# Block sums of w_in and w_out formed, split and stored from one 8 KB buffer each, stores issued by ScalarE

## The chip, the cores and the metric

One core of a Trainium2 chip runs the whole kernel in one launch. The metric is the device time of an execution in microseconds (us), lower is better. TensorE (PE in the profile, PEld for its weight loads) multiplies, VectorE (DVE) and ScalarE (ACT) do the arithmetic between, SyncE (SP, its queue SPq) only issues transfers. ScalarE can issue transfers too: such a row stands as ACTq, and ScalarE does nothing else while it issues.

## The reference, cut to what matters

```python
# attention with decay lam per head, in blocks of 64 positions, gives x: 3072 tokens x 512
def _moe_ref(x, w_in, w_out):            # w_in 512 x 2048, w_out 2048 x 512
    h = x @ w_in
    g = np.maximum(h, 0.0) + np.log1p(np.exp(-np.abs(h)))     # softplus
    return g @ w_out
```

Everything is float32. The kernel keeps that precision by splitting each operand into a high part (float32r, which TensorE multiplies in one pass) and a low remainder, so a product is three matmuls: high by high, high by low, low by high.

## The kernel before, in words

The sequence is cut into six chunks of 128 positions, 512 columns each over the four batches. Chunks 0 and 1 run `x @ w_in` and `g @ w_out` plainly. Chunks 2 and 3 (the first pair) and chunks 4 and 5 (the last pair) use a seven-product scheme in place of eight block products: P1 to P7 multiply sums of blocks of x by sums of blocks of w_in. The last pair does that for w_out too. So the weights are wanted as blocks and as four sums of blocks.

**Where the sums are made.** The sums of w_in for block i (0 to 7, each covering two 128-wide slices of the 2048) go to DRAM as g1 and g2: blocks 0 to 5 are made during chunk 1, blocks 6 and 7 in steps 0 and 1 of the first pair (`block_sums` L514, `store_sums` L528, `send_sums` L573). The sums of w_out for block i are made in step i of the first pair from the tile `w2_tiles[i]` and go to DRAM as v_sums (in the profile vP), four tables that the last pair reads: `out_block_sums` L542 forms them, `out_block_high` L555 copies the high part on ScalarE, `out_block_low` L561 subtracts it on VectorE, `send_out_sums` L568 issues four stores.

**Buffers.** `t8` (L51) hands out 21 buffers of 8 KB per partition by rotation; a tile takes a buffer that an earlier tile had, and its first writer waits until that tile's last reader is through, which for a stored tile means that the store has landed. An att unit, a w1a or w1b (`load_w1` L580, read by the products), a w2 (`load_w2` L586, read by the second matmul and by the sums) and an lb tile (activations kept for chunk 3) come from the same pool. Before, a w_out block takes two of them: `full2` for the sum of the parts and the four block sums (L544), and `parts2` for high and low (L557).

**Order of work.** `tc.manual_schedule()`: each engine runs its instructions in the order in which the Python code issues them, and waits on semaphores. In one step i of the first pair (L776 to L835) TensorE runs P1, P6, P5, P2, P7, two pieces of the second matmul of the step before (`rest`), P4, P3, four pieces of `rest`, one attention unit (`event` L677), the rest of `rest`. The tile b of P6 is taken by VectorE (u2, L796) before P7 adds to the same bank, and taken again (u3, L809) before P4 does. So P7 waits for L796 and P4 for L809. Between L796 and L809 the code puts the high and low parts of the block of the step before (L798, L799), in steps 1 and 2 also those of a w_in block (L801). After the event VectorE forms the sums of step i (L828), in steps 0 and 1 also those of a w_in block (L830). The stores stand on SyncE's queue among the loads (L827, L832).

After step 7 comes the second chunk of the pair (L836 to L869): for f from 0 to 15 four pieces of the second matmul on TensorE, while ScalarE and VectorE split the kept activations two f ahead (`split` L837, high part L631 on ScalarE, low part L635 on VectorE) and prepare the blocks of x for the last pair (L596, L597). `finish` (L648) copies an output bank on ScalarE and issues its store there.

A step's time is the stretch between the starts of P1 in the trace: step 1 is 252.2 to 275.6 us, then 275.6, 297.8, 315.7, 332.9, 361.4, 379.2 start steps 2 to 7, and the second chunk runs from 393.9 to 439.0.

Of the kernel before, what the change touches and what calls it, by code (L numbers as in the profile page):

```python
# [7 lines left out]
F32 = mybir.dt.float32  # L8
# [12 lines left out]
DM = H * D  # L21
# [11 lines left out]
def decay_attention_softplus_ffn(  # L33
# [17 lines left out]
    def t8(shape, dt, name):  # L51
        return sb.tile(shape, dt, tag="b8", bufs=21, name=name)
# [192 lines left out]
    def w_of(f, which):  # L245
        j, i = divmod(w_order.index((f, which)), 2)
        return w_pairs[j][:, :, i]
# [280 lines left out]
    def store_sums(i):  # L528
        sums = block_parts.pop(i)
        parts = t8([128, 2, 4, 256], F32R, f"parts{i}")  # L530
        nc.scalar.copy(out=parts[:, 0], in_=sums)
        nc.vector.tensor_sub(out=parts[:, 1], in0=sums, in1=parts[:, 0])
        ready[i] = parts.bitcast(F32)
# [3 lines left out]


    v_sums = {p: dr.tile([128, NF // 2, 2, 256], F32, name=f"v{p}", tag=f"v{p}") for p in ("P5", "P6", "P7", "P3")}
    out_parts = {}  # L540

    def out_block_sums(i):  # L542
        w = w2_tiles[i]
        box = t8([128, 4, DM], F32, f"full2_{i}")  # L544
        full, s1, s2, s3, s4 = box[:, 0:2], *[box[:, 2 + n // 2, n % 2 * 256 : n % 2 * 256 + 256] for n in range(4)]
        nc.vector.tensor_add(out=full, in0=w[:, :, 0], in1=w[:, :, 1])
        a11, a21 = full[:, 0, 0:256], full[:, 0, 256:512]
        a12, a22 = full[:, 1, 0:256], full[:, 1, 256:512]
        nc.vector.tensor_add(out=s1, in0=a21, in1=a22)
        nc.vector.tensor_sub(out=s3, in0=a11, in1=a21)  # L550
        nc.vector.tensor_sub(out=s2, in0=s1, in1=a11)
        nc.vector.tensor_sub(out=s4, in0=a12, in1=s2)
        out_parts[i] = [box]

    def out_block_high(i):  # L555
        box = out_parts[i][0]
        parts = t8([128, 2, 4, 256], F32R, f"parts2_{i}")  # L557
        nc.scalar.copy(out=parts[:, 0].rearrange("q n c -> q (n c)"), in_=box[:, 2:4].rearrange("q n c -> q (n c)"))
        out_parts[i].append(parts)

    def out_block_low(i):  # L561
        box, parts = out_parts[i]
        nc.vector.tensor_sub(
            out=parts[:, 1].rearrange("q n c -> q (n c)"), in0=box[:, 2:4].rearrange("q n c -> q (n c)"),
            in1=parts[:, 0].rearrange("q n c -> q (n c)"),
        )

    def send_out_sums(i):  # L568
        parts = out_parts.pop(i)[1].bitcast(F32)
        for n, p in enumerate(("P5", "P6", "P7", "P3")):  # L570
            nc.sync.dma_start(out=v_sums[p][:, i], in_=parts[:, :, n])

    def send_sums(i):  # L573
        parts = ready.pop(i)
        nc.sync.dma_start(out=g1[i][:, :, 2:4], in_=parts[:, :, 0:2])
        nc.sync.dma_start(out=g2[i][:, :, 1:3], in_=parts[:, :, 2:4])
# [194 lines left out]
    nxt = 4 * NP + 1  # L771
    for c in range(STD, NCH - 2, 2):
        more = True
        lb = {}
        gs = {}
        for i in range(NF // 2):  # L776
            unit = nxt if more else None
            if unit is not None:
                load_upto(unit + 2)
            if i + 1 < NF // 2:  # L780
                load_w1(i + 1)
            load_w2(i)
            if unit is not None and unit < NG:
                k_decay(unit)
                q_decay(unit)
            if i % 2 == 0:
                l4 = t8([128, 4, 512], F32, f"lb{c}_{i}")
            for n in range(2):
                lb[2 * i + n] = l4[:, 2 * (i % 2) + n]
            ta, tb = t4([128, 2, 512], F32, f"ta{c}_{i}"), t4([128, 2, 512], F32, f"tb{c}_{i}")  # L790
            p1, u2, u3, c21 = ta[:, 0], ta[:, 1], tb[:, 0], tb[:, 1]
            a, b_ = bank(f"a{c}_{i}"), work(f"b{c}_{i}")[:, 0]
            product("P1", i, a)
            nc.scalar.copy(out=p1, in_=a)
            product("P6", i, b_)
            nc.vector.tensor_add(out=u2, in0=b_, in1=p1)  # L796
            if i >= 1:
                out_block_high(i - 1)  # L798
                out_block_low(i - 1)  # L799
            if 1 <= i <= 2:  # L800
                store_sums(NF // 2 - 3 + i)  # L801
            c_ = bank(f"c{c}_{i}")
            product("P5", i, c_)
            product("P2", i, a, False)
            la = tl([128, 512], F32, f"la{c}_{i}")
            nc.scalar.activation(la, a, AF.Softplus)
            ga = parts_of(f"g{c}_{2 * i}", la)
            product("P7", i, b_, False)
            nc.vector.tensor_add(out=u3, in0=b_, in1=p1)  # L809
            nc.vector.tensor_add(out=u3, in0=c_, in1=u3)  # L810
            nc.scalar.activation(lb[2 * i + 1], u3, AF.Softplus)
            low_of(ga, la)
            run(rest, 2)
            product("P4", i, b_, False)
            nc.vector.tensor_add(out=c21, in0=b_, in1=p1)
            nc.scalar.activation(c21, c21, AF.Softplus)
            gb = parts_of(f"g{c}_{2 * i + 1}", c21)
            product("P3", i, c_, False)
            nc.vector.tensor_add(out=u2, in0=c_, in1=u2)
            nc.scalar.activation(lb[2 * i], u2, AF.Softplus)  # L820
            run(rest, 4)
            if unit is not None and unit <= NG:
                event(unit)
                nxt += 1
            low_of(gb, c21)
            if i >= 2:
                send_out_sums(i - 2)  # L827
            out_block_sums(i)  # L828
            if i < 2:
                block_sums(NF // 2 - 2 + i)  # L830
            if 2 <= i <= 3:
                send_sums(NF // 2 - 4 + i)  # L832
            run(rest)
            pair = [(2 * i + n, (ga, gb)[n], w2_tiles[i][:, n]) for n in range(2)]
            rest = seconds(c, pair, i == NF // 2 - 1)  # L835
# [11 lines left out]
        if more:  # L847
            steps = [lambda n=n, m=m: x_block(n, xr[c + 2][:, m + (2 if n == "P2" else 0)], m) for n in ("P1", "P2") for m in range(2)]
            for n in range(2):
                steps += [lambda n=n: x_diff(c + 2, n), lambda n=n: x_diffs(c + 2, n)]  # L850
                for ps_ in (("P5", "P6"), ("P7", "P4", "P3")):
                    steps += [lambda n=n, ps_=ps_: [x_part(p, c + 2, n) for p in ps_]]
        send_out_sums(NF // 2 - 2)
        for f in range(NF - 2):
            if f == 1:
                out_block_high(NF // 2 - 1)
                out_block_low(NF // 2 - 1)
            if f == 3:
                send_out_sums(NF // 2 - 1)
            if f % 2 == 0 and f // 2 + 2 < NF // 2:  # L860
                load_w2(f // 2 + 2)
            if f + ahead < NF:
                split(f + ahead)
            if f >= 1:
                run(steps, 1)
            if f == 9 and more:
                load_w1(0)
            run(seconds(c + 1, [(f, gs.pop(f), w2_tiles[f // 2][:, f % 2])]))
# [218 lines left out]
```

## Time and profile before

| | |
|---|---|
| time, median of 3 runs | 604.32 us (603.61 to 604.48) |
| the profiled execution | 603.4 us, of it the span of instructions 601.5 us |
| busy in the span | TensorE 571.7, VectorE 393.8, ScalarE 276.9 us |
| transfers | 148.64 MB, mean 247 GB/s |
| granted TensorE clock, mean | 0.986 |

A row of the waits names an engine and line, what it waited for, the total in us, how many times, and the longest. A row of the chain or of a timeline begins with the start in us and the length in us. A row of groups gives the count, then the shortest, median and longest duration in ns, then the first and last start. A row by windows gives the stretch, its length, the busy time of each engine, the granted clock, the share of time in which the DMA engines were busy, and GB/s.

### The profile page before, as it was taken

Reading aid. Unit: us, or ns where it says so; the run is one execution under the profiler, and the core shown is the slowest. Engines: PE = TensorE matmul, PEld = TensorE weight load, DVE = VectorE, ACT = ScalarE, POOL = GpSimd, SP = SyncE. Lnnn points to the kernel's source line nnn. Section 1 sums busy time; section 2 is a strip of 40 time slices with the busy share of each in tenths; the row PEclk is TensorE's granted clock in tenths of the full one; section 3 lists DMA queues with packets and bytes.
Section 4 is the critical chain, followed back from the end, with each engine's and each line's share of the span. In section 5 each row is a group of like instructions: output and inputs, shape, how many; then the busy total and the mean of one; then the engine's idle time right before and its main releaser. Section 6 shows DMA issues by size and latency. Waiting matters only on the chain.

```text
span 601.5 us, 12196 instructions
## 1 busy us (share of the span) xinstructions
PE 571.7 (95%) x5155; PEld 463.7 (77%) x5155; DVE 393.8 (65%) x612; ACT 276.9 (46%) x446; POOL 4.6 (1%) x11
## 2 busy tenths in 40 slices
PE   8899999999999999977999669999999999999997
PEld 6577778788888887856878557888888888788886
DVE  7779998966567775667556436659313465757983
ACT  3777766844354453533343143355213343454441
POOL 3000000000000000000000000000000000000000
PEclk9999999999999999989899979999999999999999
DMA  8998556798999766748797727969945426920801
GB/s 295 405 406 301 173 207 194 267 333 326 348 395 375 243 231 233 239 172 285 246 318 283 252 82 233 305 217 370 419 148 214 151 98 207 371 118 22 294 35 70
DMA packets 52534, 148.64 MB, mean 247 GB/s; under 512 B 4480, under 2 KB 20864, under 8 KB 46464
## 3 DMA queue, kind: packets, MB, share of 16 engines
q1 hardware_dynamic: 50176, 143.68, 67.1%
q10 hardware_dynamic: 2304, 4.20, 1.9%
q8 instruction: 40, 0.66, 0.4%
q14 instruction: 14, 0.11, 0.1%
HBM read 110.10 MB, written 37.75 MB: 246 GB/s over the span
## 4 chain that ended last, share of the span: by engine, by line
PE 77%; DVE 12%; DMA 4%; ACT 3%; issue 2%; SPq 1%; DVEq 0%; ACTq 0%
PE o L643 16%; PE rP L1014 13%; PE b L624 10%; PE h L422 10%; PE o L443 8%; PE c L624 7%; PE a L624 6%; PE x L312 2%; DMA vP<-parts 2%; PE z L327 2%; DVE c L236 2%; DVE w L243 2%; PE z L331 2%; DVE c L230 2%; DMA out_dram<-ob 1%
## 5 line engine op out<-in xcount | busy, mean ns | idle before, releaser
L643 PE MATMUL o<-w,g 128*128 128x512 f32 x432 | 104.8, 395 | 0.0
L422 PE MATMUL h<-x,w 128*128 128x512 f32 x384 | 94.9, 396 | 3.1 <-DVE w L243 2.1
L643 PEld LDWEIGHTS o<-w,g 128*128 128x128 f32 x432 | 81.2, 189 | 17.3
L422 PEld LDWEIGHTS h<-x,w 128*128 128x128 f32 x384 | 70.8, 188 | 21.1 <-DVE w L243 3.8
L443 PE MATMUL o<-w,g 128*128 128x512 f32 x336 | 82.0, 392 | 1.1 <-DVE w L243 0.8
L1014 PE MATMUL rP<-sP,vP 128*128 128x512 f32 x336 | 76.3, 389 | 0.0
L443 PEld LDWEIGHTS o<-w,g 128*128 128x128 f32 x336 | 62.4, 188 | 15.0 <-DVE w L243 1.1
L1014 PEld LDWEIGHTS rP<-sP,vP 128*128 128x128 f32 x336 | 63.1, 188 | 13.1
L624 PE MATMUL b<-xcP,w1b 128*128 128x512 f32 x192 | 52.4, 410 | 17.6 <-DVE tb L809 11.9
L624 PEld LDWEIGHTS b<-xcP,w1b 128*128 128x128 f32 x192 | 37.1, 197 | 28.4 <-DVE tb L809 13.3
L624 PE MATMUL a<-xcP,w1a 128*128 128x512 f32 x192 | 48.7, 389 | 0.0
L403 ACT ACTIVATE l<-h 128x512 f32<-128x512 f32 x32 | 19.1, 597 | 59.1 <-PE h L422 56.5
L624 PEld LDWEIGHTS a<-xcP,w1a 128*128 128x128 f32 x192 | 36.0, 188 | 7.6
L411 DVE TENSOR_TENSOR g<-l,g 128x512 fp32r<-128x512 f32 x32 | 22.0, 688 | 24.7 <-ACT g L407 24.6
L339 DVE TENSOR_TENSOR a<-x,mask 128x512 f32<-128x512 f32 x15 | 10.4, 691 | 38.7 <-PE x L312 20.4
L951 DVE TENSOR_TENSOR act<-b,ta 128x512 f32<-128x512 f32 x8 | 5.5, 691 | 31.1 <-PE b L624 31.1
L624 PE MATMUL c<-xcP,w1b 128*128 128x512 f32 x96 | 25.6, 403 | 0.0
L894 ACT CAST sP<-act 128x512 fp32r<-128x512 f32 x32 | 19.2, 619 | 13.0 <-PE rP L1014 6.8
L635 DVE TENSOR_TENSOR sP<-act,sP 128x512 fp32r<-128x512 f32 x32 | 20.9, 686 | 6.6 <-ACT sP L894 6.6
L624 PE MATMUL b<-xcP,w1a 128*128 128x512 f32 x96 | 24.4, 389 | 0.0
L624 PE MATMUL c<-xcP,w1a 128*128 128x512 f32 x96 | 24.4, 389 | 0.0
L344 DVE SCALAR_TENSOR_TENSOR st<-st,lam_c,y 64x256 f32<-64x256 f32 x52 | 22.9, 480 | 0.8
(132 smaller groups left out, 869.4 us busy)
## 6 DMA issues: line engine op xcount, KB each, us to landing
att<-in_att SPq DMA_DIRECT2D x48, 512.0 KB, 7.2
w<-g SPq DMA_DIRECT2D x23, 1024.0 KB, 8.0
raw<-in_wts SPq DMA_DIRECT2D x32, 512.0 KB, 10.2
w1a<-g SPq DMA_DIRECT2D x16, 1024.0 KB, 5.2
g<-w SPq DMA_DIRECT2D x24, 512.0 KB, 8.9
w1b<-g SPq DMA_DIRECT2D x16, 768.0 KB, 6.2
g<-parts SPq DMA_DIRECT2D x16, 512.0 KB, 8.6
vP<-parts SPq DMA_DIRECT2D x32, 256.0 KB, 7.1
```

The costliest lines, as they stand in the source:

```text
L230: nc.vector.scalar_tensor_tensor(out=c, in0=raw_at(ks, 1), scalar=0x80000000, in1=c, op0=ALU.bitwise_and, op1=ALU.bitwise_or)
L236: nc.vector.tensor_add(out=c, in0=c, in1=raw_at(ks, 0))
L344: nc.vector.scalar_tensor_tensor(out=to[:, :, t], in0=of[:, :, t], scalar=lam_c[r, h : h + 1], in1=u[:, :, t], op0=ALU.mult, op1=ALU.add,)
L403: nc.scalar.activation(l_tiles[s], h_tiles.pop(s), AF.Softplus)
L411: nc.vector.tensor_sub(out=g[:, 1, :], in0=l_tiles.pop(s), in1=g[:, 0, :])
L422: nc.tensor.matmul(h_tiles[s], lhsT=w[:, i, cs], rhs=x[:, j, :], start=p == 0 and n == 0, stop=p == NP - 1 and n == 2,)
L443: nc.tensor.matmul(o_tiles[c][b], lhsT=g[:, i, b * 128 : (b + 1) * 128], rhs=w[:, j], start=f == 0 and n == 0, stop=f == NF - 1 and n == 2,)
L624: nc.tensor.matmul(to, lhsT=w[:, k, n, p * 128 : (p + 1) * 128], rhs=x[:, j, p], start=start and p == 0 and m == 0, stop=p == 1 and m == 2 ...
L635: nc.vector.tensor_sub(out=g[:, 1], in0=l, in1=g[:, 0])
L643: nc.tensor.matmul(outs[c, b], lhsT=g[:, i, b * 128 : (b + 1) * 128], rhs=w[:, j], start=f == 0 and n == 0, stop=f == NF - 1 and n == 2,)
L894: nc.scalar.copy(out=g[:, 0], in_=of)
L1014: nc.tensor.matmul(to, lhsT=w[:, k, x, n * 128 : n * 128 + 128], rhs=g[:, y], start=fresh and i == 0 and m == 0, stop=i == NF // 2 - 1 and ...
```

## The change

One tile `box` of 8 KB per block replaces `full2` and `parts2` (and for the w_in blocks 6 and 7 the two 4 KB tiles and the 8 KB tile of parts). Its first half holds the sum of the weights' parts, its second half the four block sums. Then the high parts are written over the first half, and the low parts over the block sums, in place. One box is made in each step: w_in 6 and 7 in steps 0 and 1, w_out 2 to 7 in steps 2 to 7, and w_out 0 and 1, whose w2 tiles are loaded a second time for chunk 3, in f = 2 and f = 4 of the second chunk. The high and low parts of the box of step i are made in step i + 1, its stores are issued in step i + 2, now by ScalarE.

```diff
+    def box_sums(key):
+
+        which, i = key
+        box = boxes[key] = t8([128, 4, DM], F32, f"box{which}_{i}")
+        full, (s1, s2, s3, s4) = box[:, 0:2], [box[:, 2 + n // 2, n % 2 * 256 : n % 2 * 256 + 256] for n in range(4)]
+        if which:
+            w = w2_tiles[i]
+            nc.vector.tensor_add(out=full, in0=w[:, :, 0], in1=w[:, :, 1])
+            a12, a21 = full[:, 1, 0:256], full[:, 0, 256:512]
+        else:
+            for n in range(2):
+                w = w_of(2 * i + n, 0)
+                nc.vector.tensor_add(out=full[:, n], in0=w[:, 0], in1=w[:, 1])
...
+    def box_parts(key):
+        box = boxes[key]
+        hi, lo = [box[:, 2 * n : 2 * n + 2].rearrange("q n c -> q (n c)") for n in range(2)]
+        nc.scalar.copy(out=hi.bitcast(F32R), in_=lo)
+        nc.vector.tensor_sub(out=lo.bitcast(F32R), in0=lo, in1=hi)
+
+    def box_send(key):
+        which, i = key
+        parts = boxes.pop(key).rearrange("q (k n) (m c) -> q k (n m) c", k=2, m=2)
+        if which:
+            for n, p in enumerate(("P5", "P6", "P7", "P3")):
+                nc.scalar.dma_start(out=v_sums[p][:, i], in_=parts[:, :, n])
+        else:
+            nc.scalar.dma_start(out=g1[i][:, :, 2:4], in_=parts[:, :, 0:2])
+            nc.scalar.dma_start(out=g2[i][:, :, 1:3], in_=parts[:, :, 2:4])
...
         more = True
+        box_at = [(0, NF // 2 - 2), (0, NF // 2 - 1)] + [(1, i) for i in range(2, NF // 2)]
...
             if i >= 1:
-                out_block_high(i - 1)
-                out_block_low(i - 1)
-            if 1 <= i <= 2:
-                store_sums(NF // 2 - 3 + i)
+                box_parts(box_at[i - 1])
...
             if i >= 2:
-                send_out_sums(i - 2)
-            out_block_sums(i)
-            if i < 2:
-                block_sums(NF // 2 - 2 + i)
-            if 2 <= i <= 3:
-                send_sums(NF // 2 - 4 + i)
+                box_send(box_at[i - 2])
+            box_sums(box_at[i])
...
-        send_out_sums(NF // 2 - 2)
+        box_send(box_at[NF // 2 - 2])
         for f in range(NF - 2):
-            if f == 1:
-                out_block_high(NF // 2 - 1)
-                out_block_low(NF // 2 - 1)
-            if f == 3:
-                send_out_sums(NF // 2 - 1)
+            if f in (2, 4):
+                box_sums((1, f // 2 - 1))
+            if f in (1, 3, 5):
+                box_parts((1, f // 2 - 1) if f > 1 else box_at[NF // 2 - 1])
+            if f in (3, 5, 7):
+                box_send((1, f // 2 - 2) if f > 3 else box_at[NF // 2 - 1])
```

Where the instructions now stand: ScalarE between step 5 and step 6, before the change (z is the event's output bank, v and kd belong to the attention units, ta is the copy of P1, full and parts are the block's two tiles).

```order
L387 COPY xr_3811<-z_3932 128x2x4x64
L110 COPY v_3996<-att_3651 128x512
L290 ACTIVATE kd_4021<-att_3834,rp_128 128x4x64 x2
L794 COPY ta_6_4027<-a_6_4029 128x512
L558 CAST parts_5_4045<-full_5_4003 128x1024
```

The same place of the changed kernel.

```order
L387 COPY xr_3779<-z_3899 128x2x4x64
L110 COPY v_3963<-att_3620 128x512
L573 DMA vP_641<-box_3_3608 128x2x256
L573 DMA vP_642<-box_3_3608 128x2x256
L573 DMA vP_643<-box_3_3608 128x2x256
L573 DMA vP_644<-box_3_3608 128x2x256
L290 ACTIVATE kd_3988<-att_3802,rp_128 128x4x64 x2
L800 COPY ta_6_3994<-a_6_3996 128x512
L565 CAST box_5_3970<-box_5_3970 128x1024
```

Four store issues have come in ahead of kd and of the copy of P1, and the cast reads and writes one tile.

ScalarE in the second chunk from the split of f = 4 to that of f = 7, before the change (g is a split activation, lb the kept one, xcP a block of x for the last pair).

```order
L631 CAST g_4_4422<-lb_2_3284 128x512
L596 CAST xcP_4405<-xr_3027 128x512
L631 CAST g_5_4443<-lb_2_3284 128x512
L596 CAST xcP_4446<-xr_3027 128x512
L631 CAST g_6_4463<-lb_2_3284 128x512
L596 CAST xcP_4446<-xr_3027 128x512
L631 CAST g_7_4480<-lb_2_3284 128x512
```

The end of the same place in the changed kernel, from the split of f = 6 on.

```order
L636 CAST g_6_4441<-lb_2_3266 128x512
L601 CAST xcP_4418<-xr_3027 128x512
L565 CAST box_1_4433<-box_1_4433 128x1024
L573 DMA vP_641<-box_0_4384 128x2x256
L573 DMA vP_642<-box_0_4384 128x2x256
L573 DMA vP_643<-box_0_4384 128x2x256
L573 DMA vP_644<-box_0_4384 128x2x256
L636 CAST g_7_4464<-lb_2_3266 128x512
```

A cast of a box and four stores now stand between the splits of f = 6 and f = 7; the same five stand in the same way between those of f = 4 and f = 5, with box 0 cast and box 7 stored, and four stores of box 6 stand ahead of the split of f = 2.

VectorE in the second chunk of the changed kernel, from the low part of f = 5 to that of f = 6.

```order
L640 TENSOR_TENSOR g_5_4415<-lb_2_3266,g_5_4415 128x512
L602 TENSOR_TENSOR xcP_4418<-xr_3027,xcP_4418 128x512
L549 TENSOR_TENSOR box_1_4433<-w_1_4304 128x1024
L557 TENSOR_TENSOR box_1_4433<-box_1_4433 128x256
L558 TENSOR_TENSOR box_1_4433<-box_1_4433 128x256
L559 TENSOR_TENSOR box_1_4433<-box_1_4433 128x256
L560 TENSOR_TENSOR box_1_4433<-box_1_4433 128x256
L640 TENSOR_TENSOR g_6_4441<-lb_2_3266,g_6_4441 128x512
```

The five sums of box 1 are new in that place; before, only the one xcP row stood between the two splits.

More of the change, by code (lines that the diff above doesn't have):

```diff
@@ L539, in decay_attention_softplus_ffn @@
     v_sums = {p: dr.tile([128, NF // 2, 2, 256], F32, name=f"v{p}", tag=f"v{p}") for p in ("P5", "P6", "P7", "P3")}
[L540 to L548, printed above, removed]
+    boxes = {}
+    def box_sums(key):
[10 more added lines that the diff above has]
+                nc.vector.tensor_add(out=full[:, n], in0=w[:, 0], in1=w[:, 1])
+            a12, a21 = full[:, 0, 256:512], full[:, 1, 0:256]
+        a11, a22 = full[:, 0, 0:256], full[:, 1, 256:512]
         nc.vector.tensor_add(out=s1, in0=a21, in1=a22)
@@ L552, in out_block_sums @@
         nc.vector.tensor_sub(out=s4, in0=a12, in1=s2)
[L553 to L571, printed above, removed]
+    def box_parts(key):
[12 more added lines that the diff above has]
+            nc.scalar.dma_start(out=g2[i][:, :, 1:3], in_=parts[:, :, 2:4])
     def send_sums(i):
```

## The prediction

> **What bounds the kernel now.** I read the page first, then the stretches of the first pair, then TensorE's waits there, then the chain through each wait.
>
> ```profile
> span 601.5 us, 12196 instructions
> PE 571.7 (95%) x5155; PEld 463.7 (77%) x5155; DVE 393.8 (65%) x612; ACT 276.9 (46%) x446; POOL 4.6 (1%) x11
> ```
>
> TensorE is busy 95% of the span. Only its gaps, and the time in which it ran slowly, can be won. The view by windows, cut at the starts of the steps, shows steps 1 to 7 of the first pair and the second chunk.
>
> ```profile
> core 0: us, PE busy (x) PEld busy (x) DVE busy (x) ACT busy (x) POOL busy (x), PEclk, DMA share, GB/s
> 252.20:275.60 23.40, 19.37 (x195) 15.24 (x195) 14.00 (x24) 9.50 (x16) 0.00 (x0) 0.93 0.57 192
> 275.60:297.80 22.20, 19.16 (x196) 15.35 (x195) 15.26 (x27) 8.22 (x13) 0.00 (x0) 0.92 0.79 274
> 297.80:315.70 17.90, 17.68 (x180) 14.20 (x179) 11.55 (x20) 7.19 (x12) 0.00 (x0) 1.00 0.92 316
> 315.70:332.90 17.20, 17.20 (x180) 14.25 (x179) 10.68 (x18) 7.29 (x12) 0.00 (x0) 1.00 0.73 255
> 332.90:361.40 28.50, 19.23 (x180) 15.46 (x179) 10.77 (x18) 7.17 (x12) 0.00 (x0) 0.82 0.54 175
> 361.40:379.20 17.80, 17.52 (x179) 14.19 (x179) 10.70 (x18) 6.38 (x10) 0.00 (x0) 1.00 0.81 258
> 379.20:393.90 14.70, 14.70 (x126) 12.02 (x124) 11.71 (x20) 5.38 (x8) 0.00 (x0) 1.00 0.89 299
> 393.90:439.00 45.10, 45.10 (x199) 37.35 (x200) 24.78 (x40) 20.33 (x36) 0.00 (x0) 1.00 0.86 329
> ```
>
> Step 4 (315.70) is TensorE from end to end: 17.20 us. Against it steps 1, 2, 3, 5 and 6 are long by 6.2, 5.0, 0.7, 11.3 and 0.6 us, together 23.8. Step 7 and the second chunk have no gap.
>
> ```profile
> PE b L624 <- DVE tb L809: 11.9, 3, 9.3
> PE b L624 <- DVE ta L796: 5.0, 3, 3.0
> ```
>
> These are TensorE's waits on the banks of the products, from the view of waits: 16.9 us, all for the two VectorE operations that free the bank b. The other 6.9 us is slowness: in steps 1, 2 and 5 the same products took 19.37, 19.16 and 19.23 us at clocks 0.93, 0.92 and 0.82, about 2.0 us more each. What held VectorE is in the chain.
>
> ```profile
> 252.84 7.64 DMA out_dram<-ob
> 260.58 1.06 ACT parts L558
> 261.65 1.23 DVE parts L563
> 262.88 1.13 DVE parts L532
> ...
> 339.76 1.26 SPq L571
> 341.06 6.24 DMA vP<-parts
> 347.40 1.05 ACT parts L558
> ```
>
> Step 1: ScalarE's cast into the tile of parts waits until an output store out of that buffer has landed; VectorE, in order, stands behind the cast, then does two low parts, then L809. Step 5: the same cast waits for the stores of an earlier block's parts. Step 2 is different, in the timeline of VectorE and TensorE (the last row is from step 3):
>
> ```profile
> 277.24 1.22 DVE L546 TENSOR_TENSOR full<-w 128x1024 f32<-128x1024 f32 x1
> 279.97 1.29 DVE L518 TENSOR_TENSOR full<-w 128x512 f32<-128x512 f32 x2
> 283.37 0.68 DVE L796 TENSOR_TENSOR ta<-b,ta 128x512 f32<-128x512 f32 x1
> 284.11 1.68 PE L624 MATMUL b<-xcP,w1b 128*128 128x512 f32 x6 [3.04 <-DVE ta L796]
> 303.52 1.65 PE L624 MATMUL b<-xcP,w1b 128*128 128x512 f32 x6 [0.22 <-DVE ta L796]
> ```
>
> There VectorE makes two sets of sums ahead of L796, and P7 waits 3.04 us for it. With one set, in step 3, it waits 0.22.
>
> **What goes.** The in-place cast needs no second buffer, so it can't wait for a landing. A box still needs its one buffer when the sums start, a step earlier. By the addresses of the built program, the boxes take buffers of att and w1 tiles or of blocks whose stores were issued at least a step before, and TensorE is done with those tiles before the sums begin. That ends the stops of steps 1 and 5, and the short ones of 3 and 6, where the cast waited on a w1a tile. In steps 1 and 2 one set of sums goes (277.24 to 279.97, 2.73 us) and with it one low part. In step 2, L796 then ends at 283.37 + 0.68 - 2.73 = 281.3, and P7 was ready at 284.11 - 3.04 = 281.1: 0.2 to 0.3 us stays, as in step 3. So 23.8 - 0.5 = 23.3 us go, the slow time included, since it stood behind the stops.
>
> The operations cost the same in place, by the groups on the tiles full, sums and parts:
>
> ```profile
> L523 DVE TENSOR_TENSOR sums<-full x8: 424/426/427, 142.4 to 281.3; 128x256 f32<-128x256 f32 x8
> L549 DVE TENSOR_TENSOR full<-full x8: 424/425/426, 253.7 to 392.7; 128x256 f32<-128x256 f32 x8
> L558 ACT CAST parts<-full x8: 1044/1050/1057, 260.6 to 402.5; 128x1024 fp32r<-128x1024 f32 x8
> ```
>
> A sum into its own tile (L549) takes what one into another takes (L523), so I keep 1.05 us for the cast. The low part in place has no row; I take it unchanged.
>
> **What comes in, in the steps.** Four store issues per block move from SyncE to ScalarE, between the copy of v and kd. Here is the timeline between steps 4 and 5, and two batches of stores on SyncE's queue.
>
> ```profile
> 330.94 0.62 ACT L110 COPY v<-att 128x512 f32<-128x512 f32 x1
> 331.46 0.91 ACT L290 ACTIVATE kd<-att,rp 128x256 f32<-128x256 f32 x2
> 333.64 1.22 DVE L546 TENSOR_TENSOR full<-w 128x1024 f32<-128x1024 f32 x1
> 334.34 0.59 ACT L794 COPY ta<-a 128x512 f32<-128x512 f32 x1 [1.96 <-PE a L624]
> 372.82 3.56 SPq L571 DMA_DIRECT2D vP<-parts  x4
> 404.82 2.31 SPq L571 DMA_DIRECT2D vP<-parts  x4
> ```
>
> ScalarE has no row for this issue. SyncE's four took 2.31 to 3.56 us, waits included. On ScalarE they start at 331.56, and kd takes 0.91. L794 must end before P2, three products of 1.36 into the step, at 332.9 + 4.1 = 337.0. So 337.0 - 0.59 - 0.91 - 331.56 = 3.9 us are free, and even 3.56 hides: zero. If that cover were gone, each of the six steps would pay the 2.3.
>
> **What comes in, in the second chunk.** Boxes 0 and 1 of w_out are formed here, and the stores of boxes 6, 7, 0 and 1 are issued among the splits, which TensorE needs every 2.73 us (45.10 us for 198 matmuls, twelve for each f).
>
> ```profile
> 409.52 0.68 DVE L635 TENSOR_TENSOR g<-lb,g 128x512 fp32r<-128x512 f32 x1
> ```
>
> This row of VectorE's timeline is the low part of f = 7, ready at 410.2. TensorE comes to f = 7 after 114 of those matmuls, at 419.9, and to its third matmul, which reads the low part, at 420.3: a lead of 10.1 us. Ahead of it now stand three times four stores, two sets of sums and two casts, and they don't overlap: a cast waits for the sums, the stores stand behind the cast, the next split behind the stores, the next sums behind that split's low part. With s for four stores that is 3s + 2 x 2.73 + 2 x 1.05 = 7.6 + 3s. At s = 2.31, the batch that lies in this chunk, it is 14.5, so TensorE loses 14.5 - 10.1 = 4.4 us, in gaps of about a microsecond from f = 5 to f = 7. At s = 3.56 it is 8.1. Below, nothing: if the two engines do overlap more than I think, the loss is 0. I take 4.4. What the gaps do to the clock is bounded by step 3 (no loss of clock) and step 2 (2.0 us): I take 0. The Trainium skill, "TensorE: Matmul & The Clock Gate", section "What's actually happening", says that the clock falls to half after an idle window of some 3.4 us; by it gaps of a microsecond cost no clock, and the sum stays at 4.4.
>
> **The sum.** 603.4 - 23.3 + 4.4 = 584.5 us for the profiled execution; it lies 0.9 below the median of the runs, 604.32, so 585.4 there. About 0.2% (1.2 us) can be told from no change.
>
> **The rivals.** *The second chunk covers it all.* ScalarE stood idle there 24.8 of 45.1 us, and its stores may issue faster than SyncE's. Then 604.3 - 23.3 = 581.0. Chance 0.13.
>
> *The wait moves to the loads.* Two loads now take a box's buffer after its stores: w1b of block 6 that of box 2 (with w2 of block 5 queued behind it), w2 of block 6 that of box 3. The rows are the landing times of the stores of parts, the w2 loads among the DMA issues, and a wait of SyncE's queue in the first pair.
>
> ```profile
> DMA to landing us min/median/max: 2.8/7.1/9.7
> w<-g SPq DMA_DIRECT2D x23, 1024.0 KB, 8.0
> SPq L588 <- DMA out_dram<-ob: 11.4, 2, 10.3
> ```
>
> Stores (first row) that start 1.3 us ahead of a step are out 1.0 to 2.3 us into it, landed at 8.1 (7.1) to 12.0 (9.7), and a w2 load (second row) ends at 16.1 to 20.0. VectorE wants it at 333.64 - 315.70 = 17.9 us into the step. At the median 1.8 us are left; at the worst each of the two steps loses 2.1: 585.4 + 4.2 = 589.6, with slower stores in the second chunk 593. Chance 0.15. The Trainium skill, "DMA: Bandwidth & Descriptors", section "Issuing engines are not separate DMA queues", speaks for it and against moving the stores: all issuers share the same 16 engines, and another queue saves issue time alone. By it the landings stay as long as they were; no row of before shows stores of this kind from ScalarE.
>
> *ScalarE stands in its stores: slower.* By the built program each transfer takes one of eight completion counters in turn and is not issued until that counter's last transfer has landed. The last row shows it: a w2 load stood up to 10.3 us for an output store whose buffer it doesn't share. On SyncE that delays loads; on ScalarE it stops the casts and activations. The third store of box 3, at the end of step 5, waits for the load of att unit 23. By my times that is issued as step 4 ends, a step ahead. If SyncE ran a step late, ScalarE would stand the landing of some 7 us, less the 1.6 that the cover of 3.9 leaves beside the issue, and TensorE would restart 2.0 slow: 7.4 us in each of steps 4 to 7, 29.6 in all, and 615 us. It decides from 23.3 - 4.4 = 18.9, that is 4.7 us a step. Against it: without the stores SyncE runs further ahead. Chance 0.05.
>
> *The boxes wait as the parts did*, since their buffers come from the same rotation: 604, chance 0.03.
>
> **How the numbers follow.** My forecast has 0.64: 585.4. The low end is all 23.8 us won with nothing given back, 580.5. The high end takes s = 3.56 (8.1 us), the clock's 2.0 and both late loads (4.2): 604.3 - 23.3 + 14.3 = 595.3, rounded to 595. Outside lie the last two rivals, 0.08. Faster: 0.64 + 0.13 + 0.15 = 0.92; same 0.03; slower 0.05.
>
> **What would show it.** Right: steps 1 to 6 at 17.2 to 17.6 us with clock 1.00; no wait of a box's cast for a transfer; ScalarE's copy of P1 before P2 in every step; the second chunk at 48 to 51 us, TensorE waiting there for splits of f = 4 to 9. Wrong: a first sum or an activation that waits for a landing in steps 4 to 7, a second chunk of 45.1 or of over 54 us, or stores whose issue on ScalarE differs much from 2.3 us for four.

## The result, and the profile after

The change takes the kernel from 603.97 us (median of 4 runs, 601.45 to 604.48) to 584.71 us (4 runs, 584.27 to 585.31): a ratio of 0.969 (of the means), 95% interval 0.966 to 0.9719. The forecast was 585.4. The profiled execution took 585.31 us. In the changed kernel the line numbers differ a little: VectorE's two operations that free the bank b, formerly L796 and L809, are now L802 and L812, the products of a pair L629, the second matmuls L648, the split L636 (high, ScalarE) and L640 (low, VectorE); a box is cast at L565 and stored at L573.

The page after has a span of 583.4 us. The view by windows after, cut at the starts of the steps, with the columns as before: the first row is step 1, the last the second chunk, the one ahead of it step 7.

```profile
252.30:269.60 17.30, 17.30 (x196) 14.34 (x195) 10.35 (x18) 8.68 (x15) 0.00 (x0) 1.00 0.83 295
269.60:287.40 17.80, 17.49 (x195) 14.20 (x194) 11.55 (x21) 7.27 (x12) 0.00 (x0) 1.00 0.59 209
287.40:305.20 17.80, 17.58 (x179) 14.22 (x179) 11.51 (x20) 7.41 (x13) 0.00 (x0) 1.00 0.79 278
305.20:322.40 17.20, 17.20 (x179) 14.26 (x179) 10.69 (x18) 6.72 (x11) 0.00 (x0) 1.00 0.48 175
322.40:339.70 17.30, 17.30 (x180) 14.33 (x179) 10.78 (x18) 7.16 (x12) 0.00 (x0) 1.00 0.81 290
339.70:356.90 17.20, 17.20 (x179) 14.26 (x178) 10.65 (x17) 7.40 (x12) 0.00 (x0) 1.00 0.67 230
356.90:371.60 14.70, 14.70 (x126) 12.03 (x124) 11.71 (x20) 5.38 (x8) 0.00 (x0) 1.00 0.87 325
371.60:420.90 49.30, 47.27 (x199) 36.74 (x200) 32.37 (x52) 22.22 (x38) 0.00 (x0) 1.00 0.83 293
```

Steps 1 to 6 add up to 104.6 us where they took 127.0, with the clock at 1.00 in each: 22.4 us won. The second chunk takes 49.3 where it took 45.1: 4.2 us lost. The difference, 18.2, is the difference of the spans to 0.1 (601.5 - 583.4 = 18.1). What TensorE still waits for from step 0 to the end of the second chunk, in the view of waits (total, times, longest):

```profile
PE o L648 <- DVE g L640: 1.2, 2, 0.9
PE o L648 <- ACT g L636: 0.9, 1, 0.9
PE b L629 <- DVE ta L802: 0.5, 2, 0.3
```

The old waits of 11.9 us for L809 are gone, and of the 5.0 for L796 0.5 is left, in steps 2 and 3. New are waits of the second matmuls for splits. TensorE's own timeline of the second chunk shows where (one f has twelve of these matmuls; the row at 371.53 begins with thirty that belong to the chunk before, and the stretch holds f = 0 to 13):

```profile
371.53 12.54 PE L648 MATMUL o<-w,g 128*128 128x512 f32 x54
384.95 6.46 PE L648 MATMUL o<-w,g 128*128 128x512 f32 x26 [0.88 <-ACT g L636]
391.69 6.30 PE L648 MATMUL o<-w,g 128*128 128x512 f32 x24 [0.28 <-DVE g L640]
398.86 22.05 PE L648 MATMUL o<-w,g 128*128 128x512 f32 x94 [0.87 <-DVE g L640]
```

It stops at f = 2, at the third matmul of f = 4 and at the third of f = 6. The visible gaps add up to 2.0 us. The rest of the 4.2 lies inside the rows (47.27 us busy for what took 45.10). There the weight loads of these matmuls show it, in the view of their waits:

```profile
PEld o L648 <- DVE g L640: 3.3, 5, 1.3
```

With another 2.0 us for high parts, in three waits, the loads stood 5.3 us for splits; loads run beside matmuls (37.35 us of them beside 45.10 in the second chunk before), so TensorE loses less than that. With SyncE's stores (below) the same view has no wait for a split.

ScalarE, in the view of its waits, never waits for a landing before a box's cast. It waits for VectorE's sums:

```profile
ACT box L565 <- DVE box L560: 17.6, 9, 3.1
```

### The profile page after: what moved, and what is told of

The parts are those of the page before. It is cut to its first block, busy times and chain, and to the rows that moved or that the text cites. A ratio compares the mean times of both kernels' runs of the same rounds, so it can differ in the third digit from the quotient of the medians.

```text
span 583.4 us, 12175 instructions
## 1 busy us (share of the span) xinstructions
PE 567.5 (97%) x5155; PEld 460.1 (79%) x5155; DVE 394.3 (68%) x612; ACT 277.7 (48%) x446; POOL 4.1 (1%) x11
## 4 chain that ended last, share of the span: by engine, by line
PE 74%; DVE 10%; DMA 9%; ACT 2%; ACTq 2%; issue 1%; SPq 1%; DVEq 0%
PE rP L1014 13%; PE o L648 13%; PE b L629 11%; PE h L422 10%; PE o L443 9%; PE c L629 7%; PE a L629 7%; DMA raw<-in_wts 5%; DMA g<-w 2%; PE x L312 2%; PE z L327 2%; DMA att<-in_att 2%; ACTq L573 2%; PE z L331 1%; DVE c L236 1%
## 5 line engine op out<-in xcount | busy, mean ns | idle before, releaser
L648 PE MATMUL o<-w,g 128*128 128x512 f32 x432 | 105.8, 394 | 2.0 <-DVE g L640 1.2
L648 PEld LDWEIGHTS o<-w,g 128*128 128x128 f32 x432 | 79.9, 188 | 21.8 <-DVE g L640 3.3
L629 PE MATMUL b<-xcP,w1b 128*128 128x512 f32 x192 | 49.1, 391 | 1.3 <-DVE act L951 0.8
L629 PE MATMUL a<-xcP,w1a 128*128 128x512 f32 x192 | 48.8, 389 | 0.0
L629 PEld LDWEIGHTS b<-xcP,w1b 128*128 128x128 f32 x192 | 35.8, 188 | 9.9 <-DVE ta L802 1.4
L629 PEld LDWEIGHTS a<-xcP,w1a 128*128 128x128 f32 x192 | 36.1, 188 | 7.5
L640 DVE TENSOR_TENSOR sP<-act,sP 128x512 fp32r<-128x512 f32 x32 | 20.9, 686 | 6.6 <-ACT sP L894 6.6
L629 PE MATMUL c<-xcP,w1b 128*128 128x512 f32 x96 | 24.4, 390 | 0.0
L629 PE MATMUL b<-xcP,w1a 128*128 128x512 f32 x96 | 24.4, 389 | 0.0
L629 PE MATMUL c<-xcP,w1a 128*128 128x512 f32 x96 | 24.4, 389 | 0.0
L387 ACT COPY xr<-z 128x512 f32<-128x512 f32 x16 | 9.4, 585 | 30.4 <-PE z L331 30.0
```

Source lines behind the costliest of these rows:

```text
L629: nc.tensor.matmul(to, lhsT=w[:, k, n, p * 128 : (p + 1) * 128], rhs=x[:, j, p], start=start and p == 0 and m == 0, stop=p == 1 and m == 2 ...
L640: nc.vector.tensor_sub(out=g[:, 1], in0=l, in1=g[:, 0])
L648: nc.tensor.matmul(outs[c, b], lhsT=g[:, i, b * 128 : (b + 1) * 128], rhs=w[:, j], start=f == 0 and n == 0, stop=f == NF - 1 and n == 2,)
```

## The experiments

My theory: the stops of steps 1 to 6 went because no cast takes a second buffer, and because one set of sums went from steps 0 and 1. The 4.2 us given back are the stores that ScalarE now issues and the two boxes formed among the splits. The rivals: the other queue made the gain; VectorE's sums alone make the loss; each batch of stores costs its own gap; ScalarE stands for landings.

All runs in one table. The last two columns are differences of starts in TensorE's timeline, of the first product of step 1, of step 7 and of the second pair. In the changed kernel these are 252.17, 356.75 and 420.75 us, and they are read in the same way from each of the other traces.

| kernel | median, us (runs) | steps 1-6 | step 7 and second chunk |
|---|---|---|---|
| before | 603.97 (4) | 127.0 | 59.8 |
| the change | 584.71 (4) | 104.6 | 64.0 |
| the change again, one run | 584.68 (1) | 104.6 | 63.2 |
| all box stores on SyncE | 581.70 (4) | 104.5 | 59.8 |
| all box stores on GpSimd | 582.07 (5) | 104.6 | 59.8 |
| last boxes later | 581.53 (4) | 104.5 | 59.8 |
| SyncE and later | 581.42 (5) | 104.6 | 59.8 |
| stores of boxes 5, 6 on SyncE | 581.58 (4) | 104.6 | 59.8 |
| stores of boxes 7, 0, 1 on SyncE | 583.09 (4) | 104.6 | 61.0 |
| stores of boxes 2, 3, 4 twice | 594.01 (6) | 116.1 | 63.6 |
| before, w_out in place | 589.03 (4) | 111.0 | 59.8 |
| before, all sums in place | 587.23 (5) | 110.7 | 59.8 |

The kernel before, run beside the experiments, had medians of 603.44, 603.10 and 603.62.

**The stores back on SyncE.**

```diff
-                nc.scalar.dma_start(out=v_sums[p][:, i], in_=parts[:, :, n])
+                nc.sync.dma_start(out=v_sums[p][:, i], in_=parts[:, :, n])
```

(and the two stores of w_in's boxes likewise).

> The changed kernel with every box store issued by SyncE again instead of ScalarE; nothing else differs. My theory: the stops of steps 1 to 6 ended because no cast waits for a landing any more, and the 4.2 us of the second chunk are mostly ScalarE's issuing, four batches of stores of 2.3 to 3.7 us among the splits. Then the seven steps keep their sum of 104.6 us, and the second chunk falls from 49.3 to 45.2-46.5 us, since two sets of sums and two casts (7.6 us) fit in the lead of 10.1 us: 580.7-582 us. Rival one, the other queue made the gain: with the stores on SyncE again the loads behind them come late, the steps grow by several us, 588 us or more. Rival two, VectorE's sums and the casts make the second chunk long and the issuing costs nothing: 584.7 us, the chunk at 49.

Measured: 581.70 us, ratio 0.9643 (0.963 to 0.9656). The steps are unchanged, and the second chunk is one row of TensorE's timeline, without a gap:

```profile
371.78 45.18 PE L648 MATMUL o<-w,g 128*128 128x512 f32 x198
```

So the queue made none of the gain in the steps, and both sets of sums and all casts fit in the second chunk when ScalarE issues nothing for them. Both rivals fall. The move to ScalarE, taken alone, cost 3.0 us.

**Before, with w_out's sums in place.**

```diff
-        parts = t8([128, 2, 4, 256], F32R, f"parts2_{i}")
-        nc.scalar.copy(out=parts[:, 0].rearrange("q n c -> q (n c)"), in_=box[:, 2:4].rearrange("q n c -> q (n c)"))
+        hi, lo = [box[:, 2 * n : 2 * n + 2].rearrange("q n c -> q (n c)") for n in range(2)]
+        nc.scalar.copy(out=hi.bitcast(F32R), in_=lo)
...
```

(the low part and the four stores use the same two halves).

> The kernel before with one thing of the change: the high and low parts of w_out's blocks are written into the block's own buffer, so that no second 8 KB buffer is taken. The two sets of sums in steps 0 and 1, the separate buffers of the two w_in blocks and SyncE's stores stay as before. My theory: the waits of ScalarE's cast for a landing go with the buffer, so the stops of steps 3, 5 and 6 go (0.7 + 11.3 + 0.6 us) and most of step 1's 6.2; step 2 keeps its wait for the two sets of sums (3.0 us and 2.0 of slow clock), and step 1 some 1 to 2 us; the second chunk stays at 45.1. Then 604.0 - 12.6 - 4.5 = 587 us, between 585 and 589. But the parts of the two w_in blocks still take a buffer of their own in steps 1 and 2: if their cast waits as w_out's did, step 1 keeps its whole stop and it is 591. Rival, the other queue or the order of the work made the gain: the steps stay as they were, 600 us or more.

Measured: 589.03 us, ratio 0.9764 (0.975 to 0.9779), at the upper edge of the 585 to 589 that I expected. Steps 1 and 2 took 20.9 and 20.7 us, step 3 17.8, steps 4 to 6 17.2 each. TensorE's timeline shows the waits left in steps 1 and 2, and ScalarE's the casts of step 1, that of w_out's block and that of a w_in block's parts. In this kernel L793 and L806 are the two operations that free the bank b.

```profile
260.33 1.65 PE L621 MATMUL b<-xcP,w1b 128*128 128x512 f32 x6 [1.73 <-DVE ta L793]
264.66 1.65 PE L621 MATMUL b<-xcP,w1b 128*128 128x512 f32 x6 [1.32 <-DVE tb L806]
282.50 1.66 PE L621 MATMUL b<-xcP,w1b 128*128 128x512 f32 x6 [3.04 <-DVE ta L793]
```

```profile
256.24 1.05 ACT L558 CAST full<-full 128x1024 fp32r<-128x1024 f32 x1 [0.65 <-DVE full L552]
261.70 1.05 ACT L531 CAST parts<-sums 128x1024 fp32r<-128x1024 f32 x1 [4.41 <-DMA att<-in_att]
```

The cast in place (L558) starts as soon as its sums are there. The cast beside it, which still takes a second buffer (L531), stands 4.41 us for a landing. (The row names the transfer that landed last; by the built program the cast waits for the four output stores out of the buffer that it takes.) The two forms of the same work, in one step of one kernel, show the mechanism. The 11.3 us that step 5 was long are gone with the second buffer alone, without anything else of the change.

**Before, with all sums in place.** The order and the queue of before, with the changed kernel's box functions.

```diff
-                out_block_high(i - 1)
-                out_block_low(i - 1)
+                box_parts((1, i - 1))
             if 1 <= i <= 2:
-                store_sums(NF // 2 - 3 + i)
+                box_parts((0, NF // 2 - 3 + i))
```

> The kernel before with all block sums of the first pair formed, split and stored in one buffer each, the two of w_in too, but in the order of before: two sets of sums in steps 0 and 1, two parts in steps 1 and 2, every store from SyncE. The run with w_out alone in place (589.0) kept 3.6 us in step 1 and 3.5 in step 2; in step 1 TensorE waited 1.7 us behind the double sums and 1.3 behind the cast of the w_in parts, which stood for a landing. My theory: the second wait goes with the buffer, the first and that of step 2 (3.0 us) stay, since they are VectorE's work: 587-588.5 us. Against the run with SyncE's stores and one block a step (581.7) it prices the two sets of sums at 5.5-7 us. Rival: the landing was all of it and VectorE's second set of sums hides: 582-583 us.

Measured: 587.23 us, ratio 0.9728 (0.9707 to 0.975). The view of TensorE's waits has one line left of those on b:

```profile
PE b L629 <- DVE ta L802: 4.9, 3, 3.0
```

The wait behind the w_in cast went with its buffer, and the three waits for VectorE's work stay, 1.6 us in step 1, 3.0 in step 2 and 0.2 in step 3. Between this kernel and the one with one block a step and SyncE's stores lie 587.2 - 581.7 = 5.5 us, the price of the two double sets.

**The last boxes later.**

```diff
-            if f in (2, 4):
-                box_sums((1, f // 2 - 1))
+            late = {5: (1, 0), 9: (1, 1)}
+            if f in late:
+                box_sums(late[f])
```

(cast one f later, stored three f later; the stores of box 7 stay at f = 3).

> The changed kernel with the last two boxes formed later in the second chunk, at f = 5 and 9 instead of 2 and 4 (cast one f later, stored three later); ScalarE still issues the stores. My theory: the chunk's loss is work ahead of splits that come soon after. The gap at f = 2, 1.0 us behind the stores of the sixth box, stays; most of the other 3.1 us goes, as the splits by then lie further ahead: 581.5-583 us. Rival: the loss is the total of what ScalarE and VectorE have to do there, wherever it stands, or contention of the stores with the loads: 584.7 us.

Measured: 581.53 us, ratio 0.9643 (0.9628 to 0.9658). The whole loss is gone, the gap at f = 2 too, which I had expected to stay. The rows of the changed kernel and then of this one, on ScalarE's queue at the head of the second chunk, show the batches of box 5 and box 6 and the split of f = 2:

```profile
371.67 3.76 ACTq L573 DMA_DIRECT2D vP<-box  x4
380.56 3.68 ACTq L573 DMA_DIRECT2D vP<-box  x4
384.28 0.62 ACT L636 CAST g<-lb 128x512 fp32r<-128x512 f32 x1 [4.13 <-issue]
```

```profile
371.71 2.90 ACTq L573 DMA_DIRECT2D vP<-box  x4
379.73 2.69 ACTq L573 DMA_DIRECT2D vP<-box  x4
382.46 0.62 ACT L636 CAST g<-lb 128x512 fp32r<-128x512 f32 x1 [3.14 <-issue]
```

ScalarE's instructions up to there are the same in both; the same eight stores took 1.9 us less here, and the split came 1.8 us earlier.

**Both edits.**

> The changed kernel with both edits: all box stores issued by SyncE, and the last two boxes formed at f = 5 and 9. My theory: nothing is left ahead of the splits that TensorE waits for, the second chunk takes 45.1-45.5 us and the whole 580.5-581 us, faster than both kernels. If the stores on SyncE hold the loads of the second chunk or of the pair after it, it is slower than the run with later boxes alone.

Measured: 581.42 us, ratio 0.964 (0.9627 to 0.9653), a little above what I expected. Nothing more than either edit alone gives, since each alone already leaves the second chunk without a gap, and no slower: SyncE's stores held up no load that TensorE waited for.

**One half of the chunk's stores on SyncE, then the other.**

```diff
+        dma = nc.sync.dma_start if key in ((1, 5), (1, 6)) else nc.scalar.dma_start
...
-                nc.scalar.dma_start(out=v_sums[p][:, i], in_=parts[:, :, n])
+                dma(out=v_sums[p][:, i], in_=parts[:, :, n])
```

The other kernel has (1, 7), (1, 0) and (1, 1) in that list instead.

> The changed kernel with the stores of boxes 5 and 6, the two batches at the head of the second chunk, issued by SyncE; those of boxes 7, 0 and 1 stay on ScalarE. My theory: the loss of 4.2 us is one chain. ScalarE's split of f = 2 stands behind the second batch, VectorE stands 7.5 us for that split, and with it wait the sums of boxes 0 and 1. Without the two batches VectorE goes on several us earlier and the three later batches fit: the chunk takes 45.1-46 us, 581-582 us in all. Rival, each batch costs its own gap: only the gap of 1.05 us at f = 2 goes, the chunk takes 48.2 and the whole 583.7 us.

> The other half: the stores of boxes 7, 0 and 1 issued by SyncE, those of boxes 5 and 6 on ScalarE. My theory: the gap at f = 2 stays (up to 1.05 us); behind it VectorE starts late with the sums of box 0 and the low parts, but ScalarE's casts no longer stand behind three batches of 2.3 us, so the rest of the loss falls to 0-1 us: 581.5-583 us. Rival, VectorE's late start at f = 2 alone makes the loss: 584.7 us, as the change.

Measured: 581.58 us without the batches of boxes 5 and 6 on ScalarE (0.9634, 0.9616 to 0.9653), 583.09 without those of boxes 7, 0 and 1 (0.9662, 0.9642 to 0.9681). In the first, three batches of stores stand among the splits as in the changed kernel, and TensorE's second chunk is one row of 198 matmuls again, as long as with SyncE's stores. In the second, TensorE has no gap at f = 2, where I had expected it to stay, and one at the third matmul of f = 6:

```profile
372.03 24.28 PE L649 MATMUL o<-w,g 128*128 128x512 f32 x104
396.83 21.61 PE L649 MATMUL o<-w,g 128*128 128x512 f32 x94 [0.52 <-DVE g L641]
```

The loss is 4.2 us with all five batches, 0 without the first two, 1.2 without the last three. So it is one chain, and not a price per batch: the prices alone, 0 and 1.2, don't add up to 4.2. The batches of boxes 5 and 6 make the split of f = 2 late, VectorE starts its low part late, and with it everything that stands behind it in order. What the chain has to spare is worked out further down.

**The stores of boxes 2, 3 and 4 twice.**

```diff
                 nc.scalar.dma_start(out=v_sums[p][:, i], in_=parts[:, :, n])
+                if 2 <= i <= 4:
+                    nc.scalar.dma_start(out=v_twice[p][:, i], in_=parts[:, :, n])
```

> The changed kernel with the four stores of boxes 2, 3 and 4 issued twice by ScalarE, the second time into DRAM tiles of their own that nothing reads; these issues stand at the ends of steps 4, 5 and 6. My prediction gave ScalarE 3.9 us free there before the copy that TensorE needs. Four stores take 2.0 to 2.7 us in the changed kernel's steps, eight 4.0 to 5.5, so 0.1 to 1.6 us stick out in each of steps 5, 6 and 7: 585-589 us. Rival one, the cover is larger and another wait ends last: 584.7. Rival two, ScalarE then stands for completion counters, whose eight are taken by eight stores in a row: a landing of 3 to 7 us in each of the three steps, 593 us or more.

Measured: 594.01 us, ratio 0.9848 (0.9818 to 0.9878), where I had expected 585 to 589. The profile is that of the slowest of its six runs (597.37; the others lie between 591.8 and 596.9). ScalarE's queue between steps 4 and 5, and TensorE's wait behind it:

```profile
320.58 0.39 ACTq L574 DMA_DIRECT2D vP<-box  x1
321.01 0.48 ACTq L576 DMA_DIRECT2D dP<-box  x1
321.53 0.52 ACTq L574 DMA_DIRECT2D vP<-box  x1
322.09 0.56 ACTq L576 DMA_DIRECT2D dP<-box  x1
322.68 1.27 ACTq L574 DMA_DIRECT2D vP<-box  x1
323.99 1.08 ACTq L576 DMA_DIRECT2D dP<-box  x1
325.11 0.82 ACTq L574 DMA_DIRECT2D vP<-box  x1
328.56 0.37 ACTq L576 DMA_DIRECT2D dP<-box  x1
328.97 0.91 ACT L290 ACTIVATE kd<-att,rp 128x256 f32<-128x256 f32 x2 [7.30 <-DMA dP<-box]
```

```profile
PE a L632 <- ACT ta L803: 6.4, 2, 3.2
330.40 1.93 PE L632 MATMUL a<-xcP,w1a 128*128 128x512 f32 x6 [3.24 <-ACT ta L803]
```

Eight stores take 8.4 us (320.58 to 328.93), not the 4.0 to 5.5 expected. The fifth to seventh took two to three times as long to issue as the first two, and the eighth was held from 325.93 to 328.56. By the built program it waits for the completion counter of the third, issued at 321.53, and so for that one's landing, 7 us after its issue. This is the second rival's mechanism, in one of the eight, and the slow issues are the rest. In the next step no store is held so, and the eight take 8.3 us all the same (343.01 to 351.31). ScalarE stands 7.3 us; the prediction had given it 3.9 free, which leaves 3.4 for TensorE, and TensorE waited 3.24, here and once more in the next step, and ran slowly behind both.

**The stores on GpSimd, and the change again.** The first has `nc.gpsimd.dma_start` in the place of `nc.scalar.dma_start`, the second no edit.

> The changed kernel with every box store issued by GpSimd, which is 1% busy; nothing else differs. My theory: the second chunk lost its 4.2 us because the splits stand behind the stores on ScalarE, so any queue on which no split stands gives it back: steps as in the changed kernel, second chunk at 45.1, 581-582 us. Rival: SyncE's queue does it better than another one, because GpSimd's stores take longer to issue or to land and hold the buffers of the loads: 583-590 us.

> The changed kernel once more, for a second profile. In the first one the two batches of stores at the head of the second chunk took 3.76 and 3.68 us, and TensorE waited 0.88 us for the split of f = 2; in two kernels with the same code up to there (later boxes; last stores on SyncE) the batches took 2.90 and 2.69, and 2.17 and 2.93, and there was no such wait. If the length of a batch depends on what the two edits changed behind it, this profile repeats 3.7 us and the wait; if it varies from run to run, the batches here differ from 3.7 by several tenths, and the second chunk's loss lies anywhere between 3 and 4.2 us.

Measured: 582.07 us with GpSimd's stores (0.9645, 0.9618 to 0.9673), with the same steps and the same second chunk as with SyncE's. Its split of f = 2 shows what the batches of boxes 5 and 6 do in the changed kernel, where it stands at 384.28 (above):

```profile
379.79 0.62 ACT L636 CAST g<-lb 128x512 fp32r<-128x512 f32 x1 [0.41 <-ACT ob L656]
```

It comes 22.9 us after the start of step 7 (356.88), in the changed kernel 27.5 (356.75): 4.6 us earlier.

The change again took 584.68 us in its one run. Its batches at the head of the chunk, and TensorE's row at the first stop:

```profile
371.80 3.54 ACTq L573 DMA_DIRECT2D vP<-box  x4
380.46 2.69 ACTq L573 DMA_DIRECT2D vP<-box  x4
390.61 6.25 PE L648 MATMUL o<-w,g 128*128 128x512 f32 x24 [0.27 <-DVE g L640]
```

The same program issued the batch of box 6 in 2.69 us instead of 3.68, and that of box 5 in 3.54 instead of 3.76. There is no gap at f = 2; the stops lie at f = 4, 6 and 7, and the loss is 3.4 us instead of 4.2. So the length of box 6's batch varies from run to run, and the gap at f = 2 belongs to the long one. The batch of box 5 was long in both profiles of this program, and shorter in the two kernels that differ from it only further on (2.90 and 2.17); whether that is chance stays open.

## Why the prediction was right, and where it was not

**What goes: right, 22.4 us for 23.3.** The steps on which nothing was left came out at 17.2 to 17.3 us. Steps 2 and 3 keep 0.6 us each, not 0.2 to 0.3: behind the wait of 0.3 the six matmuls of P7 took 1.66 us for the 1.52 of other steps, and the weight loads ahead of them stood 0.7. Step 3 before, 0.7 us long with a wait of 0.22, had shown that such a wait costs more than itself. The two causes are now priced apart: w_out's second buffer 127.0 - 111.0 = 16.0 us, the second sets and w_in's buffer 6.5. Of these 6.5 the buffer alone has 1.8 by the medians (589.0 - 587.2) and 0.3 by the two profiles: step 1 became 1.6 us shorter, and step 2 happened to run 1.2 us slower, at a clock of 0.92 (last section). One booking was off: the prediction put all of step 1's 6.2 us down to the cast. With no cast waiting, step 1 still took 19.3 us, so 2.1 of them were the second set of sums.

**The operations in place: right.** The cast of a box and its low part, grouped over the ten boxes, took 1.05 and 1.22 us, as in two buffers:

```profile
L565 ACT CAST box<-box x10: 1045/1052/1057, 255.5 to 398.2; 128x1024 fp32r<-128x1024 f32 x10
L566 DVE TENSOR_TENSOR box<-box x10: 1214/1222/1226, 256.6 to 399.3; 128x1024 fp32r<-128x1024 f32 x10
```

**The stores in the steps: right.** The steps are as long with ScalarE's stores as with SyncE's or GpSimd's, and the run with the stores doubled found the 3.9 us of cover to within 0.2 (7.3 - 3.9 = 3.4 us expected of the wait, 3.24 measured).

**The second chunk: the sum right, 4.4 for 4.2 and 3.4, the working partly wrong, and the closeness luck.** The prediction put 7.6 + 3 x 2.31 = 14.5 us of work ahead of the low part of f = 7. Measured from the start of step 7, that low part was ready at 31.2 us before (410.20 - 379.04). These are its rows with all stores on SyncE, with boxes 5 and 6 on SyncE, and in the change; their step 7 starts at 357.00, 357.39 and 356.75:

```profile
395.22 0.69 DVE L640 TENSOR_TENSOR g<-lb,g 128x512 fp32r<-128x512 f32 x1
397.22 0.69 DVE L641 TENSOR_TENSOR g<-lb,g 128x512 fp32r<-128x512 f32 x1 [0.97 <-ACT g L637]
401.27 0.69 DVE L640 TENSOR_TENSOR g<-lb,g 128x512 fp32r<-128x512 f32 x1 [0.73 <-ACT g L636]
```

So it came 7.8, 9.4 and 14.1 us later than before. The total of 14.5 is nearly met, its parts are not:

- *The two boxes, 7.6 forecast, 7.8 measured.* The two casts run beside VectorE and cost nothing. In their place stand two low parts on VectorE, some 1.1 us each, which the sum had left out.
- *The batches of boxes 7 and 0, 4.6 forecast, 1.6 measured* (9.4 - 7.8). Here "they don't overlap" failed. An issue begins while the cast before it still runs (last section), and VectorE had other work meanwhile: it stood only 0.5 and 1.0 us for the two splits behind them. By the prediction's rule these two batches alone would lose 2 x 2.31 + 7.6 - 10.1 = 2.1 us; with boxes 5 and 6 on SyncE nothing is lost.
- *The batch of box 6, 2.3 forecast, 3.7 measured,* and the split of f = 2 stands behind all of it. The prediction took one length for every batch, and had named issues that differ much from 2.3 us as a sign of being wrong.
- *The batch of box 5, not counted, 0.9 measured* of its 3.76 us, since most of it fell into time in which ScalarE waits for TensorE's output banks anyway; a batch of 2.90 or 2.17 at that place (boxes later; last stores on SyncE) delayed the split of f = 2 by nothing.

The lead of 10.1 us is what the chain has. The boxes take 7.8 of it, so 2.3 are left; the batches make f = 7 another 6.3 us late (14.1 - 7.8), and 4.0 are lost, where 4.2 were measured. With the batches of boxes 7, 0 and 1 on SyncE the place that decides is f = 6. Its lead before, reckoned like that of f = 7, was 8.6 us. Two sums and one low part take 6.6 of it, and a split of f = 2 that is 3.0 us late then loses 1.0, where 1.2 were measured. The gaps were placed from f = 5 to f = 7; they came at f = 2, 4 and 6 in one profile and at 4, 6 and 7 in the other.

The profiled execution, for which the sum gave 584.5, took 585.3 us. Less was won in the steps, by 0.9, and 0.2 less was lost in the chunk.

**The clock: right.** The gaps of up to 0.9 us left it at 1.00.

**The rivals.** The second chunk did not cover it all, but would have with any one of four small edits. No box's cast and no first sum waited for a late load. The landings of the stores didn't stay as long as they were, as the prediction had them for that rival: their median is 4.3 us, against 7.1 before and 5.7 with SyncE's stores, at other moments each time. ScalarE was not stopped in the steps by completion counters; the run with the stores doubled shows that it can be, at some 5 to 6 us a step (step 5 took 22.4 us there, step 6 23.6), where the prediction had reckoned 7.4.

**What is faster than both kernels.** Five of the kernels: their medians lie between 581.4 and 582.1 us, and their slowest run, 582.58, is under the fastest of the changed kernel, 584.27. They can't be told apart. The one with the smallest edit leaves the boxes where the change has them and issues all their stores on SyncE.

**What stays open.** Why a batch of four stores takes 2.2 us to issue in one run and 3.7 in another. The wait for a landing was taken away only together with the second buffer; a second buffer of the parts' own, which would end the wait with no other edit, wasn't tried.

## What to carry to other kernels

A cast that takes a fresh buffer from a shared rotation waits for whatever transfer last read that buffer, and everything behind it in its engine's order waits too; look whether the result fits where its input stands. Put a store on the engine on whose queue nobody waits just then: the same issues cost nothing in the steps, where ScalarE had some 3.9 us free, and 3 to 4 us in the chunk, where its next instruction was a split that TensorE wanted. When an order of work gives back part of a gain, find the first late instruction of the chain: the two batches at its head, moved away, were worth as much as all five.

## What the runs showed of the hardware

**ScalarE's issue of a store starts while its instruction before still runs.** In the changed kernel's second chunk the issue starts 0.07 us into a cast of 1.05:

```profile
391.06 1.05 ACT L565 CAST box<-box 128x1024 fp32r<-128x1024 f32 x1 [3.14 <-DVE box L560]
391.13 2.36 ACTq L573 DMA_DIRECT2D vP<-box  x4
393.53 0.62 ACT L636 CAST g<-lb 128x512 fp32r<-128x512 f32 x1 [1.42 <-DMA vP<-box]
```

Those stores are box 7's, which didn't need that cast. ScalarE stood idle 1.42 us for a batch of 2.36. So the text ahead of the prediction is too strict in saying that ScalarE does nothing else while it issues: what stands ahead runs on, and only the next instruction waits. In the steps the issue even passes an instruction: between steps 4 and 5 of the changed kernel the first store of box 2 starts at 319.95 us, the copy of v that stands ahead of it in the order at 320.42.

**The length of an issue varies alike on ScalarE and on SyncE, and hardly at all on GpSimd.** The stores of one kind, min, median and max in ns, in the changed kernel (ScalarE), with the stores on SyncE, and with the stores on GpSimd:

```profile
L573 ACTq DMA_DIRECT2D vP<-box x32: 366/518/2306, 319.9 to 403.3; - x32
```

```profile
L573 SPq DMA_DIRECT2D vP<-box x32: 360/488/1612, 305.0 to 396.9; - x32
```

```profile
L573 POOL DMA_DIRECT2D vP<-box x32: 707/719/739, 294.7 to 398.9; - x32
```

The issue of a single store of 256 KB takes from 0.37 to 2.3 us on ScalarE's queue, from 0.36 to 1.6 on SyncE's, and 0.71 to 0.74 on GpSimd. The Trainium skill, "Perfetto Trace Analysis", section "DMA Instruction — HWDGE (DVE, Sync)", says that the profiled length holds a wait for the descriptor generator beside the generating itself. The spread on ScalarE and SyncE would fit that, but no view of these runs shows the two apart.

**The same wait may or may not cost clock.** Step 2 has the wait of 3.04 us in the run with w_out in place and in the one with all in place. These are its windows in the two:

```profile
273.90:294.60 20.70, 17.66 (x196) 14.11 (x195) 15.26 (x27) 8.24 (x13) 0.00 (x0) 1.00 0.86 292
```

```profile
271.50:293.40 21.90, 18.86 (x196) 15.20 (x195) 15.40 (x27) 8.23 (x13) 0.00 (x0) 0.92 0.83 276
```

In the first the clock stayed at 1.00 and the products took 17.66 us; in the second it fell to 0.92 and they took 18.86, the six matmuls right behind the wait 2.93 us instead of 1.66. The Trainium skill, "TensorE: Matmul & The Clock Gate", section "What's actually happening", says that the window of some 3.4 us over which activity is watched runs freely, and that the moment at which the clock changes depends on where in it the first matmul lands. The two rows would fit that, though no view shows where the window stood. They also show that a gap somewhat shorter than the window can be enough. A shorter one was, in step 1 before: TensorE stood 2.31 us there up to 264.67 us, and in windows of 2 us from 264 on the clock was 0.78, 0.50 and 0.87, and 1.00 again from 270.
